# Loads, turns and visits at other places in the order of a linear-attention and feed-forward kernel

## The chip, the cores and the metric

The kernel runs on one core of one Trainium2 chip. The metric is device time in microseconds. A core has TensorE (PE, matmuls), VectorE (DVE), ScalarE (ACT), GpSimd (POOL) and SyncE (SP), each with an instruction stream of its own that it executes in order, and DMA queues that POOL, SP and ACT issue to. Matmuls write to PSUM.

## The reference

Linear attention with decay, in blocks of 64 positions (batch 4, 8 heads, 768 positions, head size 64), and behind it a feed-forward layer on 3072 tokens (512 to 2048 to 512):

```python
intra = np.einsum('bhic,bhjc->bhij', qb, kb) * Dmask[None]
intra = np.einsum('bhij,bhjd->bhid', intra, vb)
inter = np.einsum('bhid,bhde->bhie', qb * lam_pow[None], kv_state)
out[:, :, sl] = intra + inter
kv_state = lam_block[None, :, None, None] * kv_state + np.einsum('bhsd,bhse->bhde', kb_dec, vb)
...
h = x @ w_in
sp = np.where(h > 20.0, h, np.log1p(np.exp(np.minimum(h, 20.0))))
g = h * np.tanh(sp)
return (g @ w_out).astype(np.float32)
```

x is the attention's output, with the heads of a position side by side.

## The kernel before

The kernel cuts the positions into blocks of 128. A chunk is one batch's block with all eight heads; chunk i has block n = i // 4 and batch i % 4, so there are 24 chunks, four to each of six blocks. A block's four chunks together are 512 tokens. For each chunk k, q and v are loaded from DRAM as 16-bit numbers by POOL (`load_k` L70, `load_q` L85, `load_v` L88). The decay is folded into the keys and into the output: `scale_k` (L306) multiplies the keys by a power of the decay, on POOL for chunks 4 to 19, and writes `ktil`.

The chunks are turned (transposed) in two ways. For chunks 0 to 7, `first_t` transposes on TensorE (L228); ScalarE copies the keys out (`pkT`, L237) and VectorE the queries (`pqT`, L246). Then `first_s` computes scores (L262) and masks, and `first_o` the output. From chunk 8 on, `turn` scales on POOL and has SP issue two DMA transposes (L315), which write `qraw` and `kraw`. Such chunks are taken two at a time, as a pair, in a visit: `pair_s` has the scores (L367) and the part of the output that comes from the state (L373); VectorE masks the scores (L382). Some units later `pair_o` has the rest of the output (L394), VectorE empties it (`xtok`, L400), and SP issues transposes of it into `xt` (L404), the input of the feed-forward layer. `pair_a` brings the state up to date: `state_half` for each two chunks (L331), VectorE adds the old state, POOL multiplies by the decay (`wc`, L347).

The feed-forward layer is dense work for TensorE, cut into units of four wide matmuls. For a block, `mm1_unit` (L423) makes one of 16 slices of h in a `ph` buffer of PSUM and ScalarE applies the activation (`hsg`, L430). `mm2_unit` (L455) is a quarter of one batch's output in a `po` buffer; after the fourth, ScalarE copies it to `osb` (L473) and issues the write to DRAM. `ph` and `po` have two buffers each; `pS`, `pk`, `pO`, `pq` one.

The order is written out by hand. First come chunks 0 to 3 and the 16 mm1 units of block 0, with chunks 4 to 7 between them at the units that a table `steps` gives (L556). Then block 1's mm1 work is done in tiles by chunk (L441), with more of chunks 4 to 7 and the turn of chunk 8; then chunks 9 to 11 are turned. The loop of L583 follows. Its first turn, n = 1, is the double period: 32 units, the mm2 units of blocks 0 and 1. Each further turn, n = 2 to 5, has the 16 mm1 units of block n and then its 16 mm2 units. Between the units of a turn stand the two visits of block n + 1 (visit 0 for its chunks 0 and 1, visit 1 for its chunks 2 and 3), and the loads and turns of block n + 2, each put by `at(u, ...)` behind unit u. In the double period the visits are at units 9 and 16, their second steps at 13 and 20.

`behind` is a copy of one element on POOL (`tick`, L411). It reads what a unit has produced, and since POOL executes in order, what follows it on POOL is not issued before that unit has come so far. Semaphores between producers and consumers are put in by the framework.

Of the kernel before, what the change touches and what calls it, by code (L numbers as in the profile page):

```python
# [13 lines left out]
def bc(ap, axis, n):  # L14
    shape = list(ap.shape)
    shape.insert(axis, n)
    return ap.unsqueeze(axis).broadcast_to(shape)
# [3 lines left out]
def kernel(  # L21
# [11 lines left out]
    B, H, S, D = q.shape  # L33
# [6 lines left out]
    NKI = DF // 128  # L40
# [3 lines left out]
    NT = 2  # L44
# [27 lines left out]
    def load_q(i):  # L72
        if i == 0:
            qn[i] = const.tile([128, H, D], F32, name="qn0")
            nc.scalar.dma_start(out=qn[i], in_=chunk_rows(q, i))
            return
        if i < B:
            qn[i] = const.tile([128, RS, D], F16, name=f"qn{i}")
            n, b = divmod(i, B)
            nc.gpsimd.dma_start(  # L80
                out=qn[i].rearrange("p r c -> p (r c)"),
                in_=q[b, :, n * C : (n + 1) * C, :].rearrange("h (s r) c -> h s (r c)", r=RS))
            return
        qn[i] = loads.tile([128, H, D], F16, name="qn", tag="qn")
        nc.gpsimd.dma_start(out=qn[i], in_=chunk_rows(q, i))  # L85
# [23 lines left out]
    def win_t(ni, kc):  # L109
        w = DF // WS // 128  # L110
        t, o = (win0[min(ni, 2)], max(ni - 2, 0)) if ni < w else (win[ni // w], ni % w)
        return t[:, kc, o * 128 : o * 128 + 128]
# [211 lines left out]
    def state_half(n, h, spare, bufs=2):  # L324

        pv = ps.tile([128, 2, JP, D], F32, name="pv", tag=spare, bufs=bufs)
        for x in range(2):
            i = n * B + 2 * h + x
            for j in range(JP):
                for t in range(2):  # L330
                    nc.tensor.matmul(  # L331
                        pv[64 * t : 64 * t + 64, x, j, :], ktil[i][:, 2 * j + t, :],
                        vz[i % NVB][:, 2 * j + t, 0:D], start=True, stop=True)
        rows = [slice(64 * t, 64 * t + 64) for t in range(2)]
        own = [wst[rs, 2 * h : 2 * h + 2, :, rs] for rs in rows]
        if n == 0:
            for rs, o in zip(rows, own):
                nc.vector.tensor_tensor(
                    out=o, in0=pv[rs], in1=bc(bc(lbc[rs, :], 1, 2), 3, D), op=ALU.mult)
            return  # L340
        raw = work.tile([128, 2, JP, D], F32, name="raws", tag="raws", bufs=2)
        if n == 1:
            for rs, o in zip(rows, own):
                nc.vector.tensor_tensor(out=raw[rs], in0=pv[rs], in1=o, op=ALU.add)
        else:
            nc.vector.tensor_tensor(out=raw, in0=pv, in1=wcp[h][n % 2], op=ALU.add)  # L346
        nc.gpsimd.tensor_tensor(  # L347
            out=wcp[h][(n + 1) % 2], in0=raw, in1=bc(bc(lbc, 1, 2), 3, D), op=ALU.mult)
# [61 lines left out]
    def behind(src):  # L410
        nc.gpsimd.tensor_copy(tick, src)  # L411

    hsg = [None] * NG
# [3 lines left out]
    def mm1_part(n, ni, lo, hi):  # L417

        if lo == 0:
            ph_t[ni] = ps.tile([128, GT], F32, name="ph",  # L420
                               tag="ph", bufs=2)
        for kc in range(NKC):
            nc.tensor.matmul(ph_t[ni][:, lo:hi], win_t(ni, kc), xt[n][:, kc, lo:hi],  # L423
                             start=(kc == 0), stop=(kc == NKC - 1))

    def mm1_unit(n, ni):
        if hsg[n] is None:
            hsg[n] = work.tile([128, NKI, GT], F16, name="hsg", tag="hsg", bufs=2)
        mm1_part(n, ni, GT - C if ni in ph_t else 0, GT)
        nc.scalar.activation(hsg[n][:, ni, :], ph_t.pop(ni), AF.Mish)  # L430
# [29 lines left out]
    last_out = [None]  # L460
# [66 lines left out]
    first_s(3)  # L527
    busy(2)
    mm1_part(0, 0, 0, GT - C)
    first_o(3)  # L530
    mm1_part(0, 1, 0, GT - C)
    scale_k(0)
    scale_k(1)
# [19 lines left out]
    load_wout(3)  # L553
    load_k(2 * B)
    load_q(2 * B)
    steps = {11: ((first_t, 4),), 13: ((first_s, 4),), 14: ((first_t, 5), (first_o, 4)), 15: ((first_s, 5),)}  # L556
    for u in range(NKI):
        mm1_unit(0, u)
        if u in (1, 3):
            state_half(0, u // 2, "po")  # L560
        if u == 6:
            nc.vector.tensor_scalar(out=maskT, in0=rel, scalar1=0.0, scalar2=None, op0=ALU.is_ge)
        if u in (6, 7, 8, 10):
            i = {6: 4, 7: 5, 8: 6, 10: 7}[u]
            nc.vector.memset(vz[i][:, :, D : 2 * D], 0.0)
        for f, c in steps.get(u, ()):
            f(c)
    g = 2 * B
    for c in (g + 1, g + 2, g + 3):
        load_k(c)  # L570
        load_q(c)
    steps = {(4, 0): ((first_t, 6),), (4, 1): ((first_o, 5), (first_s, 6)), (4, 2): ((first_t, 7),),
             (4, 3): ((first_o, 6), (first_s, 7)), (5, 1): ((first_o, 7),),
             (6, 1): ((state_half, 0), (turn, g)), (6, 2): ((state_half, 1),)}
    for c in range(B, 2 * B):
        for s in range(WS):
            mm1_tile(c, s)
            for f, i in steps.get((c, s), ()):
                f(*((1, i, "po") if f is state_half else (i,)))
    for f, i in ((turn, 1), (load_v, 0), (turn, 2), (load_v, 1), (turn, 3), (load_v, 2), (load_v, 3)):  # L580
        f(g + i)

    for n in range(NT - 1, NG):  # L583
        dense = [(mm2_unit, m, b, part) for m in ((0, 1) if n < NT else (n,))
                 for b in range(B) for part in range(WS)]
        if n >= NT:
            dense = [(mm1_unit, n, ni) for ni in range(NKI)] + dense
        todo = {}

        def at(u, f, *args):  # L590
            todo.setdefault(u, []).append((f, args))

        if n + 1 < NG:
            pairs = []
            for b in (0, 2):
                s = Pair()
                s.n, s.b = n + 1, b
                pairs.append(s)
            steps = (((9, pair_s, 0), (13, pair_o, 0), (16, pair_s, 1), (20, pair_o, 1),
                      (24, pair_a, 1)) if n < NT else  # L600
                     ((4, pair_s, 0), (8, pair_o, 0), (13, pair_s, 1), (17, pair_o, 1),
                      (20, pair_a, 1)))
            for u, f, b in steps:
                at(u, f, pairs[b])
        if n == NT:
            at(0, lambda: behind(hsg[n][0:1, 0, 0:1]))
            at(0, turn, (n + 1) * B + 2)
            at(0, turn, (n + 1) * B + 3)
        if n + 2 < NG:
            c = (n + 2) * B  # L610
            loads_ = [(f, c + b) for b in range(B) for f in (load_k, load_q)]
            loads_ += [(load_v, c + b) for b in range(B)]
            for x, (f, i) in enumerate(loads_):
                if n >= NT:
                    u = (1, 2, 3, 5, 6, 8, 10, 11, 12, 13, 14, 15)[x]
                    at(u, lambda u=u: behind(hsg[n][0:1, u, 0:1]))
                else:
                    u = 7 + x // 2 * 4
                    if x % 2 == 0:
                        at(u, lambda: behind(last_out[0][0:1, 0:1]))  # L620
                at(u, f, i)
            for b, u in enumerate((21, 23) if n < NT else (18, 19, 21, 23)):
                at(u, turn, c + b)
        for u, (fn, *args) in enumerate(dense):
            fn(*args)
            if u == 0 and late:
                late.pop()()
            for f2, args in todo.get(u, ()):
                if args and isinstance(args[0], Pair):
                    args[0].spare = "po" if u < NKI - 1 and n >= NT else "ph"  # L630
                f2(*args)
# [30 lines left out]
```

## Time and profile before

| | |
|---|---|
| median of three runs | 263.37 us |
| the three runs | 209.98, 263.37, 299.13 us |
| the profiled execution | 210.82 us |
| its span, first to last instruction | 209.0 us |
| TensorE busy | 202.3 us, 97% |
| POOL, ACT, DVE busy | 98.7, 87.2, 67.8 us |
| granted TensorE clock | 1.000 |

The span is shorter than the execution by what lies around it. A row in order of time gives start, length, engine, line, operation, tiles out and in, shapes, and how many were merged; idle time of the engine before it and what ended it stand in brackets. Matmuls overlap, so the time that one costs is read from start to start.

### The profile page before, as it was taken

To read this page: it belongs to the slowest core of one execution; us is meant where nothing else is said; L and a number is where in the kernel's file an instruction comes from. 1 tells how busy PE (TensorE), PEld (TensorE's weight loads), DVE (VectorE), ACT (ScalarE), POOL (GpSimd) and SP (SyncE) were. 2 spreads that over 40 slices of the span, in tenths; PEclk is the share of its full clock that TensorE was granted. 3 is DMA by queue.
4 is the path that set the end of the run, shared out by engine and by line. 5 is a ranking of instruction groups with operands and counts; after the bars stand their busy time and mean duration, and the time that the engine had idled before them with its cause. 6 is when DMAs were issued, how large, how long until landed. Compare 5 with 4: busy or idle time off the path is not lost.

```text
span 209.0 us, 4353 instructions
## 1 busy us (share of the span) xinstructions
PE 202.3 (97%) x1790; PEld 110.1 (53%) x1790; DVE 67.8 (32%) x123; ACT 87.2 (42%) x151; POOL 98.7 (47%) x143
## 2 busy tenths in 40 slices
PE   7999999999999899999999999999999999999993
PEld 4565448999545454445544455544455544444442
DVE  7679516505006522042630042681043600000000
ACT  5865666665311111456312456211556221666120
POOL 7998179944994358796873176840000000000000
PEclk9999999999999999999999999999999999999999
DMA  8999999999999999999996799997702083100112
GB/s 125 141 167 202 185 142 96 157 190 168 145 200 183 193 164 175 217 162 146 136 151 164 186 79 106 133 142 181 171 4 50 2 100 105 50 0 0 53 50 100
DMA packets 107591, 26.78 MB, mean 128 GB/s; under 512 B 99890, under 2 KB 104626, under 8 KB 107570
## 3 DMA queue, kind: packets, MB, share of 16 engines
q0 software_dynamic: 75776, 13.38, 81.8%
q1 hardware_dynamic: 27296, 6.63, 23.2%
q10 hardware_dynamic: 4498, 6.49, 9.5%
q8 instruction: 14, 0.23, 0.5%
q14 instruction: 7, 0.06, 0.1%
HBM read 27.26 MB, written 6.29 MB: 161 GB/s over the span
## 4 chain that ended last, share of the span: by engine, by line
PE 65%; POOL 15%; DMA 15%; issue 2%; SPq 1%; DVE 0%; POOLq 0%
PE po L455 33%; PE ph L423 27%; DMA kn<-in_k_dram 6%; DMA wout<-in_moe_w_out_dram 5%; DMA kraw<-ktil 4%; POOL ktil L306 4%; POOL vz L88 3%; POOL kn L70 2%; PE pS L367 2%; PE pO L394 2%; SPq L315 1%; POOL qn L85 1%; POOL win L101 1%; POOL win L104 1%; POOL wc L347 1%
## 5 line engine op out<-in xcount | busy, mean ns | idle before, releaser
L455 PE MATMUL po<-wout,hsg 128*128 128x512 f16 (+2 forms) x400 | 85.4, 371 | 0.0
L423 PE MATMUL ph<-xt,win 128*128 128x512 f16 (+2 forms) x328 | 72.7, 374 | 0.1
L455 PEld LDWEIGHTS <-hsg 128*128 128x128 f16 x400 | 37.7, 98 | 42.3
L430 ACT ACTIVATE hsg<-ph 128x512 f16<-128x512 f32 x80 | 47.7, 597 | 29.5 <-PE ph L423 29.5
L423 PEld LDWEIGHTS <-win 128*128 128x128 f16 x328 | 30.9, 98 | 35.0 <-issue 0.6
L473 ACT ACTIVATE osb<-po 128x512 f32<-128x512 f32 (+1 forms) x24 | 14.2, 593 | 75.2 <-PE po L455 65.4
L382 DVE TENSOR_TENSOR sb<-pS,maskT 128x512 f16<-128x512 f32 x32 | 20.0, 684 | 57.4 <-PE pS L367 57.4
L70 POOL DMA_DIRECT2D kn<-in_k_dram x23 | 20.9, 907 | 6.9 <-issue 2.3
L88 POOL DMA_DIRECT2D vz<-in_v_dram x24 | 21.7, 905 | 2.0 <-DMA win<-in_moe_w_in_dram 1.0
L85 POOL DMA_DIRECT2D qn<-in_q_dram x20 | 17.9, 896 | 4.9 <-DMA wout<-in_moe_w_out_dram 3.5
L306 POOL TENSOR_TENSOR ktil<-kn,lk 128x512 f16<-128x512 f16 x16 | 16.7, 1050 | 3.8 <-DMA kn<-in_k_dram 3.7
L400 DVE TENSOR_TENSOR xtok<-pO,lqt 128x512 f16<-128x512 f32 x16 | 10.3, 687 | 16.8 <-PE pO L394 16.8
L441 PE MATMUL ph<-xt,win 128*128 128x128 f16 x256 | 15.7, 219 | 0.0
L441 PEld LDWEIGHTS <-win 128*128 128x128 f16 x256 | 14.4, 98 | 0.4
L465 DVE COPY osb<-po 128x128 f32<-128x128 f32 x1 | 0.3, 292 | 38.5 <-PE po L455 38.5
L445 ACT ACTIVATE hsg<-ph 128x512 f16<-128x512 f32 x16 | 9.6, 597 | 6.9 <-PE ph L441 6.9
L347 POOL TENSOR_TENSOR wc<-raws,lbc 128x512 f16<-128x512 f32 x8 | 8.6, 1095 | 5.2 <-DVE raws L346 5.2
L411 POOL COPY tick<-hsg 1x1 f16<-1x1 f16 x25 | 4.4, 177 | 11.7 <-ACT hsg L430 11.6
L268 DVE TENSOR_TENSOR sb<-pS,maskT 128x512 f16<-128x512 f32 x8 | 5.2, 686 | 4.9 <-PE pS L262 4.9
L176 PE MATMUL busy<-kzero 128*128 128x512 f16 x12 | 5.4, 526 | 1.2 <-DVE kzero L158 1.2
L306 DVE TENSOR_TENSOR ktil<-kn,lk 128x512 f16<-128x512 f16 (+1 forms) x8 | 6.4, 840 | 0.0
L288 PE MATMUL pO<-sb,vz 128*128 128x128 f16 x64 | 5.9, 219 | 0.3
(76 smaller groups left out, 118.2 us busy)
## 6 DMA issues: line engine op xcount, KB each, us to landing
out_dram<-osb ACTq DMA_DIRECT2D x23, 256.0 KB, 2.9
vz<-in_v_dram POOLq DMA_DIRECT2D x24, 128.0 KB, 4.7
kn<-in_k_dram POOLq DMA_DIRECT2D x23, 128.0 KB, 5.3
qn<-in_q_dram POOLq DMA_DIRECT2D x23, 128.0 KB, 5.4
wout<-in_moe_w_out_dram POOLq DMA_DIRECT2D x4, 512.0 KB, 10.1
win<-in_moe_w_in_dram POOLq DMA_DIRECT2D x3, 512.0 KB, 9.2
kn<-in_k_dram SPq DMA_DIRECT2D x1, 256.0 KB, 3.2
qn<-in_q_dram ACTq DMA_DIRECT2D x1, 256.0 KB, 3.9
```

Source lines behind the costliest of these rows:

```text
L70: nc.gpsimd.dma_start(out=kn[i], in_=chunk_rows(k, i))
L85: nc.gpsimd.dma_start(out=qn[i], in_=chunk_rows(q, i))
L88: nc.gpsimd.dma_start(out=vz[i % NVB][:, :, 0:D], in_=chunk_rows(v, i))
L306: (nc.vector if i < B or i >= (NG - 1) * B else nc.gpsimd).tensor_tensor(out=t, in0=kn[i], in1=bc(lk, 2, D), op=ALU.mult)
L347: nc.gpsimd.tensor_tensor(out=wcp[h][(n + 1) % 2], in0=raw, in1=bc(bc(lbc, 1, 2), 3, D), op=ALU.mult)
L382: nc.vector.tensor_tensor(out=s.sb[x][t], in0=pS[x][t], in1=bc(maskT, 1, JP), op=ALU.mult)
L400: nc.vector.tensor_tensor(out=xtok[:, :, :, t, :], in0=s.pO[t], in1=bc(bc(lqj[:, :, t], 1, 2), 3, D), op=ALU.mult)
L423: nc.tensor.matmul(ph_t[ni][:, lo:hi], win_t(ni, kc), xt[n][:, kc, lo:hi], start=(kc == 0), stop=(kc == NKC - 1))
L430: nc.scalar.activation(hsg[n][:, ni, :], ph_t.pop(ni), AF.Mish)
L441: nc.tensor.matmul(ph[:, u, :], win_t(w * s + u, kc), xt[n][:, kc, b * C : (b + 1) * C], start=(kc == 0), stop=(kc == NKC - 1),)
L455: nc.tensor.matmul(po[:, lo:hi], hsg[n][:, ki, b * C : (b + 1) * C], wout[part][:, kk, lo:hi], start=(ki == 0), stop=(ki == NKI - 1),)
L473: nc.scalar.activation(o, i, AF.Copy)
```

## The change

Instructions keep their kind; all but a few `tick` copies keep their number. Six things change:

- The turn of chunk 4 on TensorE (`first_t`) stands behind unit 12 of block 0, before behind unit 11.
- Unit 2 of block 0 takes its PSUM tile from the `po` buffers, before from `ph`.
- The second `state_half` of block 0 takes `pS`, before `po`.
- In the double period the loads of v for chunks 10 and 11, before issued with the turns ahead of it, stand behind the output copy of unit 11, ahead of k and q of chunk 12; k and q of chunks 13, 14 and 15 follow behind units 15, 19 and 23, v of chunks 12 and 13 behind unit 27. Before, k and q of chunk 12 stood behind unit 7. Chunk 13 is turned behind unit 24, before 23.
- In turn n = 2, chunks 14 and 15 are turned behind units 0 and 1 (before both behind 0), and their v is loaded behind unit 2 (before in the double period).
- In turns n = 2, 3 and 4, visit 0 is at units 6 and 10, before 4 and 8. In n = 2 and 3 the loads are at units 4 to 23, before 1 to 15, the last three behind output copies; the turns are at 19, 22, 25 and 28, before 18, 19, 21 and 23.

```diff
             ph_t[ni] = ps.tile([128, GT], F32, name="ph",
-                               tag="ph", bufs=2)
+                               tag="po" if n == 0 and ni == 2 else "ph", bufs=2)
...
-    steps = {11: ((first_t, 4),), 13: ((first_s, 4),), 14: ((first_t, 5), (first_o, 4)), 15: ((first_s, 5),)}
+    steps = {12: ((first_t, 4),), 13: ((first_s, 4),), 14: ((first_t, 5), (first_o, 4)), 15: ((first_s, 5),)}
...
-            state_half(0, u // 2, "po")
+            state_half(0, u // 2, *(("po", 2), ("pS", 1))[u // 2])
...
-    for f, i in ((turn, 1), (load_v, 0), (turn, 2), (load_v, 1), (turn, 3), (load_v, 2), (load_v, 3)):
+    for f, i in ((turn, 1), (load_v, 0), (turn, 2), (load_v, 1), (turn, 3)):
...
-                     ((4, pair_s, 0), (8, pair_o, 0), (13, pair_s, 1), (17, pair_o, 1),
+                     ((6, pair_s, 0), (10, pair_o, 0), (13, pair_s, 1), (17, pair_o, 1),
...
+        def after(u, *todo_):
+            if n >= NT and u < NKI:
+                at(u, lambda: behind(hsg[n][0:1, u, 0:1]))
+            else:
+                at(u, lambda: behind(last_out[0][0:1, 0:1]))
+            for f, i in todo_:
+                at(u, f, i)
+
         if n == NT:
-            at(0, lambda: behind(hsg[n][0:1, 0, 0:1]))
-            at(0, turn, (n + 1) * B + 2)
-            at(0, turn, (n + 1) * B + 3)
+            c = (n + 1) * B
+            after(0, (turn, c + 2))
+            after(1, (turn, c + 3))
+            after(2, (load_v, c + 2), (load_v, c + 3))
         if n + 2 < NG:
...
+            if n < NT:
+                after(11, (load_v, c - 2), (load_v, c - 1), (load_k, c), (load_q, c))
...
+            else:
...
+                for u, (f, i) in zip((4, 5, 7, 8, 10, 11, 13, 14, 15, 19, 19, 23), loads_):
+                    after(u, (f, i))
-            for b, u in enumerate((21, 23) if n < NT else (18, 19, 21, 23)):
+            for b, u in enumerate((21, 24) if n < NT else (19, 22, 25, 28)):
                 at(u, turn, c + b)
```

On TensorE, around unit 11 of block 0, the order before is this (`ph_557` is unit 11, `pk_563` and `pq_570` the turn of chunk 4, `ph_577` unit 12, `ph_583` unit 13, `pS_589` the scores of chunk 4; of each step one row is shown):

```order
L423 MATMUL ph_557<-xt_249,win2_81 128x512
...
L228 MATMUL pk_563<-ident_89,ktil_425 128x128
...
L228 MATMUL pq_570<-ident_89,qn_415 128x128
...
L423 MATMUL ph_577<-xt_249,win3_82 128x512
...
L423 MATMUL ph_583<-xt_249,win3_82 128x512
...
L262 MATMUL pS_589<-pqT_575,pkT_568 128x128
```

With the change, at the same place (`ph_563` is unit 12, `pk_569` and `pq_576` the turn, `ph_583` unit 13):

```order
L423 MATMUL ph_557<-xt_249,win2_81 128x512
...
L423 MATMUL ph_563<-xt_249,win3_82 128x512
...
L228 MATMUL pk_569<-ident_89,ktil_425 128x128
...
L228 MATMUL pq_576<-ident_89,qn_415 128x128
...
L423 MATMUL ph_583<-xt_249,win3_82 128x512
...
L262 MATMUL pS_589<-pqT_581,pkT_574 128x128
```

The turn has moved behind unit 12, and one unit is left between it and the scores.

On POOL, at the start of the double period, the order before is this (`ktil_1119` is the scaling of chunk 11, `vz2_71` and `vz3_72` the loads of v for chunks 10 and 11, `osb_1164` the output copy of unit 7, `osb_1235` that of unit 11, `kn_1168` and `qn_1170` are chunk 12, `kn_1239` and `qn_1241` chunk 13):

```order
L306 TENSOR_TENSOR ktil_1119<-kn_666,lk_158 128x512
L88 DMA vz2_71<-in_v_dram 128x8x64
L88 DMA vz3_72<-in_v_dram 128x8x64
L411 CAST tick_167<-osb_1164 1x1
L70 DMA kn_1168<-in_k_dram 128x8x64
L85 DMA qn_1170<-in_q_dram 128x8x64
L411 CAST tick_167<-osb_1235 1x1
L70 DMA kn_1239<-in_k_dram 128x8x64
L85 DMA qn_1241<-in_q_dram 128x8x64
```

With the change (`osb_1228` is the output copy of unit 11, `osb_1277` that of unit 15, `kn_1234` and `qn_1236` are chunk 12, `kn_1281` and `qn_1283` chunk 13):

```order
L306 TENSOR_TENSOR ktil_1119<-kn_666,lk_158 128x512
L411 CAST tick_167<-osb_1228 1x1
L88 DMA vz2_71<-in_v_dram 128x8x64
L88 DMA vz3_72<-in_v_dram 128x8x64
L70 DMA kn_1234<-in_k_dram 128x8x64
L85 DMA qn_1236<-in_q_dram 128x8x64
L411 CAST tick_167<-osb_1277 1x1
L70 DMA kn_1281<-in_k_dram 128x8x64
L85 DMA qn_1283<-in_q_dram 128x8x64
```

Four loads that stood right behind the scaling of chunk 11, two of them behind unit 7, now stand behind unit 11. The order on SP is the same as before.

More of the change, by code (lines that the diff above doesn't have):

```diff
@@ L604 @@
                 at(u, f, pairs[b])
+        def after(u, *todo_):
[5 more added lines that the diff above has]
+                at(u, f, i)
         if n == NT:
-            at(0, lambda: behind(hsg[n][0:1, 0, 0:1]))
-            at(0, turn, (n + 1) * B + 2)
-            at(0, turn, (n + 1) * B + 3)
+            c = (n + 1) * B
+            after(0, (turn, c + 2))
+            after(1, (turn, c + 3))
+            after(2, (load_v, c + 2), (load_v, c + 3))
         if n + 2 < NG:
             c = (n + 2) * B
[L611 to L621, printed above, removed]
-            for b, u in enumerate((21, 23) if n < NT else (18, 19, 21, 23)):
+            if n < NT:
+                after(11, (load_v, c - 2), (load_v, c - 1), (load_k, c), (load_q, c))
+                after(15, (load_k, c + 1), (load_q, c + 1))
+                after(19, (load_k, c + 2), (load_q, c + 2))
+                after(23, (load_k, c + 3), (load_q, c + 3))
+                after(27, (load_v, c), (load_v, c + 1))
+            else:
+                loads_ = [(f, c + b) for b in range(B) for f in (load_k, load_q)]
+                loads_ += [(load_v, c + b) for b in range(B)]
+                for u, (f, i) in zip((4, 5, 7, 8, 10, 11, 13, 14, 15, 19, 19, 23), loads_):
+                    after(u, (f, i))
+            for b, u in enumerate((21, 24) if n < NT else (19, 22, 25, 28)):
                 at(u, turn, c + b)
```

## The prediction

> **What bounds the kernel now.** I read the page first: busy shares, slices and granted clock.
>
> ```profile
> span 209.0 us, 4353 instructions
> PE 202.3 (97%) x1790; PEld 110.1 (53%) x1790; DVE 67.8 (32%) x123; ACT 87.2 (42%) x151; POOL 98.7 (47%) x143
> PE   7999999999999899999999999999999999999993
> PEclk9999999999999999999999999999999999999999
> ```
>
> TensorE is busy nearly everywhere, at the full granted clock in every slice, so a change that takes no work from it can win only its holes. The digits drop in the first slice, around slice 14, and in the last. The busy time by stages says where holes are left (columns after the stretch: length, PE, PEld, DVE, ACT, POOL, clock, DMA share, GB/s):
>
> ```profile
> 21.00:54.00 33.00, 32.51 (x452) 25.06 (x451) 13.22 (x23) 21.19 (x37) 21.93 (x25) 1.00 1.67 156
> 54.00:70.00 16.00, 15.78 (x122) 7.52 (x119) 3.96 (x7) 2.44 (x5) 11.36 (x16) 1.00 1.79 175
> 70.00:85.50 15.50, 14.80 (x133) 7.45 (x134) 4.97 (x8) 1.79 (x3) 10.99 (x15) 1.00 1.59 181
> 85.50:116.00 30.50, 30.50 (x255) 14.95 (x254) 8.83 (x14) 11.94 (x20) 20.89 (x34) 1.00 1.55 165
> 116.00:206.00 90.00, 89.84 (x628) 43.66 (x625) 20.22 (x31) 36.32 (x61) 14.71 (x26) 1.00 0.59 82
> ```
>
> From 21 to 54 us 0.49 us is idle, from 54 to 85.5 us 0.92 us, and from 85.5 to 206 us 0.16 us in 120.5. So after the double period nothing can be won, only lost. TensorE's list in order of time (start, length, then the operation) shows the two holes, and a third that the busy column hides:
>
> ```profile
> 18.02 0.44 PE L331 MATMUL pv<-vz,ktil 128*64 128x64 f16 x16
> 18.55 1.89 PE L423 MATMUL ph<-xt,win 128*128 128x512 f16 x8
> 20.37 0.44 PE L331 MATMUL pv<-vz,ktil 128*64 128x64 f16 x16
> 20.75 7.08 PE L423 MATMUL ph<-xt,win 128*128 128x512 f16 x32
> 28.32 0.40 PE L228 MATMUL pk<-ident,ktil 128*128 128x128 f16 x4 [0.49 <-POOL ktil L306]
> ...
> 28.77 1.89 PE L423 MATMUL ph<-xt,win 128*128 128x512 f16 x8
> ...
> 30.93 1.04 PE L423 MATMUL ph<-xt,win 128*128 128x512 f16 x4
> 31.80 0.39 PE L228 MATMUL pk<-ident,ktil 128*128 128x128 f16 x4
> ...
> 61.98 0.62 PE L367 MATMUL pS<-qraw,kraw 64*128 64x128 f16 x16
> 62.44 0.40 PE L373 MATMUL pO<-wc,qraw 64*128 64x64 f16 x16
> ...
> 69.38 0.40 PE L367 MATMUL pS<-qraw,kraw 64*128 64x128 f16 x8
> 70.70 0.40 PE L367 MATMUL pS<-qraw,kraw 64*128 64x128 f16 x8 [0.92 <-DMA kraw<-ktil]
> 70.94 0.40 PE L373 MATMUL pO<-wc,qraw 64*128 64x64 f16 x16
> 71.27 3.63 PE L455 MATMUL po<-wout,hsg 128*128 128x512 f16 x16
> 74.73 0.63 PE L394 MATMUL pO<-vz,sb 128*128 128x64 f16 x16
> ```
>
> Starts tell more than busy time, since matmuls overlap. Sixteen wide matmuls take from 71.27 to 74.73, 3.46 us or 0.216 us each, and a unit is four of them, 0.865 us. The 32 that start at 20.75 therefore end their issue at 27.67, and the next step starts at 28.32: 0.65 us lost, where 30.93 to 31.80 shows that this change of step alone costs nothing (four times 0.216 is 0.865 of 0.87). At 69.38, sixteen score matmuls should take the 0.46 us of 61.98 to 62.44, but the step behind them starts 1.56 us later: 1.10 us lost. From 18.02 to 18.55 is 0.53 us, where the same sixteen matmuls from 20.37 to 20.75 take 0.38: 0.15 us lost. What lies around the span is 210.82 - 209.0 = 1.82 us, and I leave it.
>
> [...] By the idle column the two marked holes are worth 0.49 + 0.92 = 1.41 us, and less the 0.11 found below the time would be 209.5; by starts they and the third are 1.90 us. [...]
>
> **Chunk 4 turned behind unit 12.** PE waits at 28.32 for POOL's scaled keys of chunk 4. POOL in turn waited for that chunk's load, and the change touches neither:
>
> ```profile
> 27.22 1.04 POOL L306 TENSOR_TENSOR ktil<-kn,lk 128x512 f16<-128x512 f16 x1 [3.72 <-DMA kn<-in_k_dram]
> 30.04 1.06 POOL L306 TENSOR_TENSOR ktil<-kn,lk 128x512 f16<-128x512 f16 x1
> 29.05 0.69 DVE L246 TENSOR_TENSOR pqT<-pq,lq 128x512 f16<-128x512 f16 x1 [5.46 <-PE pq L228]
> ```
>
> They are done at 28.26. With one more unit in front, and 0.15 us won at unit 2, PE arrives at 27.67 - 0.15 + 0.865 = 28.38, when they are ready. The 0.65 us goes. What is late next is the score step of chunk 4, which now has one unit behind the turn instead of two. The turned q is ready 29.74 - 28.32 = 1.42 us after the turn starts. PE comes there after 0.45 (28.32 to 28.77) plus 0.865, 1.31 us, so it waits 1.42 - 1.31 = 0.11 us. The next turn, of chunk 5, would start at 31.80 - 0.65 - 0.15 + 0.11 = 31.11; its keys are ready at 31.10. Term: 0.65 - 0.11 = 0.54 us, with bounds 0.4 (a little lost at chunk 5 too) and 0.65.
>
> **Unit 2 on another bank.** It takes a "po" buffer instead of the third "ph", so it need not wait until ScalarE has read unit 0. The second state half goes to the "pS" bank, which no step uses between the scores of chunk 3 and those of chunk 4. Term: 0.15 us, bounds 0 (something else holds unit 2) and 0.15.
>
> **The double period's loads and turns.** The 1.10 us is a wait for the transposed keys of chunk 11. The chain of waits, then the POOL list, then SyncE's list, then what transposes and loads took from issue to landing (the whole run's kraw; kraw, qraw, vz in their own stretches; kn from 65 to 78 us):
>
> ```profile
> 62.69 7.97 DMA kraw<-ktil
> 59.42 1.81 POOL L88 DMA_DIRECT2D vz<-in_v_dram  x2
> 61.35 0.88 POOL L70 DMA_DIRECT2D kn<-in_k_dram  x1
> 65.43 0.18 POOL L411 CAST tick<-osb 1x1 f16<-1x1 f32 x1 [2.33 <-ACT osb L473]
> 65.89 0.88 POOL L70 DMA_DIRECT2D kn<-in_k_dram  x1 [0.28 <-issue]
> 61.29 1.30 SPq L315 DMA_TRANSPOSE qraw<-qn  x1
> DMA to landing us min/median/max: 2.4/3.2/8.0
> DMA to landing us min/median/max: 4.6/5.5/7.5
> DMA to landing us min/median/max: 3.6/6.0/6.1
> ```
>
> Issued at 62.69, the transpose landed at 70.66, while v of chunks 10 and 11 (two issues from 59.42) and k, q of chunk 12 (from 61.35) were under way. The run's median for such a transpose is 3.2 us. The change puts those four loads behind the output copy of unit 11, so none is issued between the scaling of chunk 11 and about 64.7 us. SyncE's order is the same, and its issue at 62.69 follows from POOL and its own queue. At the median the keys land at 65.9; PE, earlier by 0.54 + 0.15 = 0.69 us, wants them at 69.38 + 0.23 - 0.69 = 68.92, so even 6.2 us is enough. Term: 1.10 us.
>
> What is late next is v of chunk 11, wanted by the output step that stood at 74.73. It now starts at 74.73 - 1.10 - 0.69 = 72.94, and chunk 11 is its second half, 73.17. POOL's tick behind unit 11 moves from 65.43 to 64.74; the first load starts 0.46 us behind it as now (65.43 to 65.89), v of chunk 11 is the second, 0.88 later: 66.08. That leaves 7.1 us. Loads of v from 56 to 62 us took 4.6 to 7.5 us, loads of k from 65 to 78 us 3.6 to 6.1. I take 6.0: nothing added. Behind the waiting tick on POOL stand only the loads and, ten units on, the scaling of chunk 12, so its new wait of some 5 us holds up nobody else.
>
> **Later periods.** Visit 0 two units later, turns spread to units 19 to 28, v loads behind mm2 copies: I cost them at nothing.
>
> ```profile
> 94.08 0.63 PE L394 MATMUL pO<-vz,sb 128*128 128x64 f16 x16
> 98.96 0.62 PE L367 MATMUL pS<-qraw,kraw 64*128 64x128 f16 x16
> 91.03 1.31 SPq L315 DMA_TRANSPOSE kraw<-ktil  x1
> DMA to landing us min/median/max: 5.7/5.7/5.7
> ```
>
> The tightest is chunk 15, turned early in period 2: its keys were issued at 91.03 and landed 5.7 us later, 96.7, and are wanted at 98.96, 2.2 us to spare. Its scaling now follows unit 1 rather than unit 0, but it stood second in POOL's line anyway, so it moves with PE. The last turn, behind unit 28, is wanted behind unit 13 of the next period, 17 units or 14.7 us on; scaling 1.06, two issues of 1.3 and the worst landing of 8.0 make 11.7. The visits now stand three units apart from output step 0 to visit 1, 2.6 us against the 4.9 of 94.08 to 98.96 now; VectorE must have emptied the two accumulators by then, two operations of about the 0.69 us of the pqT row. If such a cover failed it would fail in each of three periods, about 1 us each.
>
> **Sum.** 0.54 + 0.15 + 1.10 = 1.79 us; 210.82 - 1.79 = 209.03, so 209.0. The runs shown have a median of 263.37, from 209.98 to 299.13. The profiled execution stands beside the fastest, 0.4% above it, and 20% below the median; the trace, with the full clock throughout, holds nothing that would make 50 us, so the forecast is for an undisturbed execution.
>
> **Rivals.** *The transpose is late for another reason* (0.12): it is held by its own queue and by output writes, which stay. For it: SyncE issues it right behind the one of 61.29, both on one queue, and an output write leaves at that time too. Against it: the run's median of 3.2, with the same queue and the same writes. Then the keys still land at 70.66, PE resumes at 70.70 as now, and everything won before is swallowed there: 210.8.
>
> *v of chunk 11 is late* (0.08), which ends on the slower side. With a landing time L the loss is L - 7.1: nothing up to 7.1, 0.4 at 7.5, the whole gain at 8.9, and beyond that slower than before. The longest transpose under load took 8.0, giving 209.9; with L = 10 it is 211.9, and 2% slower would need L = 13. For it: four loads are queued in a row, and transposes of x compete. [...]
>
> *A cover fails in every later period* (0.04): 1 us in each of three gives 212.0, 2 us each 215.
>
> *The comparison is off by itself* (0.09), the three runs shown being as far apart as they are: 0.06 to the faster side, as the median lies far above the fastest, 0.03 to the slower.
>
> **Numbers.** The forecast's own case has the remaining 0.67, from 208.2 (the fastest run shown less the sum) to 209.5. The range is 208.0 to 211.4: it takes in the first rival with the 0.6 us or so by which executions differ, and the second up to L = 9.5; 0.67 + 0.12 + 0.05 = 0.84 lie within. A measurement of this kernel can tell about 2%, 4.2 us. Faster by that would be 206.6, which no case of the trace reaches, as all holes together give 1.90: 0.06, from the last rival. Slower, 215.0: 0.03 from it, 0.02 from late v, 0.02 from the periods: 0.07. Within: 0.87.
>
> **What would show it.** Right: no idle before the chunk 4 turn, a score step of chunk 4 that waits 0.1 us, unit 2 starting 0.38 us after the state half, no wait in visit 1 of the double period, the keys of chunk 11 landing within about 4 us, and PE without holes from there. Wrong: an idle PE at the second output step waiting for vz, at visit 1 still waiting for kraw, or small repeated holes in the periods behind.

## The result, and the profile after

| | before | changed |
|---|---|---|
| median of 16 runs | 210.16 us | 209.14 us |
| runs, lowest to highest | 209.34 to 212.01 us | 208.76 to 209.67 us |
| profiled execution | 210.82 us | 209.13 us |
| its span | 209.0 us | 207.3 us |

The ratio is 0.9948, with a 95% interval of 0.9928 to 0.9968: a gain of half a per cent, within the 2% that was called no change. Two of the 16 runs of before, 299.13 us and the 263.37 us that was the first median, are disturbed ones and are left out of the range and of the ratio, as such runs are in the ratios further down; medians are of all runs. The profiled executions lie 1.69 us apart, the medians 1.02 us. The experiments below are mostly about that difference.

On the page of the changed kernel, the summary by engine of the chain that ended last:

```profile
PE 91%; DVE 0%; issue 0%
```

The same line of the kernel before, and some of the pieces of its chain in order of time:

```profile
PE 65%; POOL 15%; DMA 15%; issue 2%; SPq 1%; DVE 0%; POOLq 0%
14.62 12.46 DMA kn<-in_k_dram
...
27.22 1.04 POOL ktil L306
28.26 0.89 POOL qn L85
...
61.29 1.30 SPq L315
...
62.69 7.97 DMA kraw<-ktil
...
70.70 0.40 PE pS L367 x8
```

From the load of chunk 4's keys to visit 1 the chain of before went over DMA, POOL and SyncE, and not over TensorE's first hole.

The changed kernel's busy time by stages (length, PE, PEld, DVE, ACT, POOL, clock, DMA share, GB/s):

```profile
21.00:54.00 33.00, 33.00 (x454) 25.32 (x453) 13.31 (x23) 21.22 (x37) 21.96 (x26) 1.00 1.66 157
54.00:70.00 16.00, 16.00 (x145) 8.04 (x144) 4.47 (x8) 2.39 (x4) 10.49 (x13) 1.00 1.61 169
70.00:85.50 15.50, 15.50 (x116) 7.43 (x114) 4.36 (x7) 2.98 (x5) 10.97 (x15) 1.00 1.90 196
85.50:116.00 30.50, 30.50 (x255) 15.01 (x254) 8.84 (x14) 11.39 (x20) 22.53 (x37) 1.00 1.91 162
```

The idle 0.49 and 0.92 us are gone: TensorE is busy without a break from 21 to 116 us, and the chain runs over TensorE alone from early on. TensorE's list in order of time, at the places of the three holes:

```profile
18.25 0.44 PE L331 MATMUL pv<-vz,ktil 128*64 128x64 f16 x16
18.62 1.90 PE L423 MATMUL ph<-xt,win 128*128 128x512 f16 x8
...
20.83 7.94 PE L423 MATMUL ph<-xt,win 128*128 128x512 f16 x36
28.61 0.39 PE L228 MATMUL pk<-ident,ktil 128*128 128x128 f16 x4
...
29.06 1.03 PE L423 MATMUL ph<-xt,win 128*128 128x512 f16 x4
30.07 0.40 PE L262 MATMUL pS<-pqT,pkT 64*128 64x128 f16 x8
...
68.87 0.62 PE L367 MATMUL pS<-qraw,kraw 64*128 64x128 f16 x16
69.33 0.40 PE L373 MATMUL pO<-wc,qraw 64*128 64x64 f16 x16
...
73.12 0.63 PE L394 MATMUL pO<-vz,sb 128*128 128x64 f16 x16
```

Unit 2 starts 0.37 us after the state half (before 0.53). The 36 matmuls from 20.83 and the turn of chunk 4 follow each other without a gap. The sixteen score matmuls of visit 1 stand in one row, 0.46 us from the step behind them (before 1.56). All of it starts 0.23 us later than before (18.25 against 18.02): the start of the kernel, which the change does not touch, took that much longer in this execution.

POOL's list and SyncE's list in the double period, then the time from issue to landing of the transposed keys of chunk 11 (issued at 63.11) and of v of chunk 11 (the second of the two issues from 65.26):

```profile
64.85 0.18 POOL L411 CAST tick<-osb 1x1 f16<-1x1 f32 x1 [4.96 <-ACT osb L473]
65.26 1.82 POOL L88 DMA_DIRECT2D vz<-in_v_dram  x2 [0.24 <-issue]
63.11 2.15 SPq L315 DMA_TRANSPOSE kraw<-ktil  x1
DMA to landing us min/median/max: 4.4/4.4/4.4
DMA to landing us min/median/max: 4.1/4.1/4.1
```

POOL now idles 4.96 us before the tick. The keys land 4.4 us after their issue in place of 8.0, at 67.5, and are wanted at 69.1 (their scores are the second half of the row at 68.87, 0.23 later). v of chunk 11 is issued at 66.2, lands at 70.3 and is wanted at 73.12 + 0.23 = 73.35: 3 us to spare.

### The profile page after: what moved, and what is told of

The parts are those of the page before. It is cut to its first block, busy times and chain, and to the rows that moved or that the text cites. A ratio compares the mean times of both kernels' runs of the same rounds, so it can differ in the third digit from the quotient of the medians.

```text
span 207.3 us, 4355 instructions
## 1 busy us (share of the span) xinstructions
PE 202.1 (97%) x1790; PEld 110.5 (53%) x1790; DVE 68.8 (33%) x123; ACT 87.0 (42%) x151; POOL 100.1 (48%) x144
## 4 chain that ended last, share of the span: by engine, by line
PE 91%; DVE 0%; issue 0%
PE po L455 40%; PE ph L423 34%; PE ph L441 7%; PE pS L367 2%; PE pO L394 2%; PE pv L331 2%; PE pO L288 1%; PE pO L373 1%; PE pS L262 1%; PE pk L228 0%; PE pO L284 0%; PE pq L228 0%; DVE osb L465 0%; DVE ktil L306 0%
## 5 line engine op out<-in xcount | busy, mean ns | idle before, releaser
L411 POOL COPY tick<-hsg 1x1 f16<-1x1 f16 x21 | 3.7, 176 | 10.2 <-ACT hsg L430 10.0
L411 POOL CAST tick<-osb 1x1 f16<-1x1 f32 x11 | 2.4, 219 | 12.7 <-ACT osb L473 12.7
L306 DVE TENSOR_TENSOR ktil<-kn,lk 128x512 f16<-128x512 f16 (+1 forms) x8 | 7.2, 944 | 0.0
```

Source lines behind the costliest of these rows:

```text
L306: (nc.vector if i < B or i >= (NG - 1) * B else nc.gpsimd).tensor_tensor(out=t, in0=kn[i], in1=bc(lk, 2, D), op=ALU.mult)
```

## The experiments

The theory: the transposed keys of chunk 11 are late because four loads are under way beside them, and while they are late, whatever TensorE wins before visit 1 is lost again there. The rivals: the keys are late for their own queue and the output writes; or each hole counts for itself and the three terms simply add. Ratios are to the kernel before, run beside each.

| kernel | median, us | ratio | 95% interval |
|---|---|---|---|
| changed, second time | 209.15 | 0.9954 | 0.9923 to 0.9984 |
| early edits alone | 211.02 | 1.0032 | 1.0000 to 1.0064 |
| the same, second time | 210.22 | 0.9989 | 0.9950 to 1.0028 |
| the same, third time | 210.54 | 0.9999 | 0.9951 to 1.0047 |
| double period's loads alone | 209.37 | 0.9955 | 0.9927 to 0.9982 |
| only k, q of chunk 12 later | 209.40 | 0.9968 | 0.9941 to 0.9995 |
| only v of 10 and 11 later | 209.36 | 0.9952 | 0.9922 to 0.9982 |
| early edits, k, q of 12 later | 209.33 | 0.9957 | 0.9932 to 0.9983 |
| changed, later periods as before | 209.24 | 0.9954 | 0.9930 to 0.9978 |
| changed, v behind unit 15 | 211.80 | 1.0078 | 1.0043 to 1.0113 |
| before, once more | 211.13 | 1.0023 | 0.9983 to 1.0064 |
| before, two output writes left out | 209.59 (one run) | | |

The kernel before against itself, 1.0023, shows what such a ratio can be without any edit.

**The early edits alone.** The kernel before with these lines:

```diff
-                               tag="ph", bufs=2)
+                               tag="po" if n == 0 and ni == 2 else "ph", bufs=2)
...
-    steps = {11: ((first_t, 4),), 13: ((first_s, 4),),
+    steps = {12: ((first_t, 4),), 13: ((first_s, 4),),
...
-            state_half(0, u // 2, "po")
+            state_half(0, u // 2, *(("po", 2), ("pS", 1))[u // 2])
```

> The kernel before with the two early edits alone: chunk 4 turned behind unit 12, unit 2 on the po buffers and the second state half on pS. Theory: holes one and three go (no idle before the turn of chunk 4, 0.37 us from state half to unit 2), TensorE reaches visit 1 of the double period 0.7 to 0.8 us earlier, but the keys of chunk 11 land when they did, so the wait there grows by what was won: its idle time 0.9 plus 0.7, and the time moves by no more than 0.3 us (209.8 to 210.2 where before has 210.16). Rival, each hole counts for itself: 0.7 us faster, 209.4, with a wait at visit 1 as before.

> The two early edits alone once more, since the first profile of them is of its slowest kind (span 211.9) and 12 runs went from 209.91 to 214.45. Theory: what TensorE wins before visit 1 is swallowed there, and more than that: loads that are tied to TensorE's units (k and q of chunk 13 behind unit 11) start earlier while the transposes of chunk 11 don't, so the keys land later. Expected: a wait of 1 to 3 us at visit 1 again, k of chunk 13 issued near 65.1 (65.89 in the kernel before), median 0 to 1 us above before. Rival, chance of that run: the wait is 0.5 to 1 us and the median is at or below before.

> The two early edits alone, for a profile like the others (the first had the longest wait of its kind, the second was disturbed as a whole). Theory: no hole at chunk 4 and none at unit 2, and a wait at visit 1 of 1 to 2 us, longer than the 0.8 and 1.1 us in the two profiles of the kernel before by about what was won ahead of it; span 208.3 to 209.3. Rival, each hole counts for itself: the wait is 1 us or less and the span at or below 208.0.

Three ratios, 1.0032, 0.9989 and 0.9999: no gain, and not the loss of up to 1 us that I expected of the second either. The second's profiled execution took 728.48 us and isn't read. In the third profile, TensorE at visit 1, and the landing of the keys issued at 62.33:

```profile
68.88 0.40 PE L367 MATMUL pS<-qraw,kraw 64*128 64x128 f16 x8
70.72 0.40 PE L367 MATMUL pS<-qraw,kraw 64*128 64x128 f16 x8 [1.45 <-DMA kraw<-ktil]
62.33 8.35 DMA kraw<-ktil
```

TensorE comes there 0.50 us earlier than before (68.88 against 69.38; 0.7 to 0.8 was expected) and goes on at 70.72, where before had 70.70: the wait grew from 0.92 to 1.45 us, just by what was won. Both holes ahead were gone, and the span is 209.0 us like before's. So the holes don't count for themselves, as the chain of before already said: it reaches visit 1 past the first of them. That the keys landed within 0.02 us of before's is luck, since they were issued 0.36 us earlier and took 0.38 us longer. The other half of my expectation stays open: in the third run k of chunk 13 was issued at 65.4, half a microsecond earlier than before, and the keys took 8.4 us in place of 8.0 but landed at 70.68, no later. In the first profile they did land later, at 72.01, after 8.6 us, but there SyncE had issued them later too, at 63.44.

**The double period's loads alone.** The changed kernel without the early edits, and with the tables of the later periods as before:

```diff
-                     ((6, pair_s, 0), (10, pair_o, 0), (13, pair_s, 1), (17, pair_o, 1),
+                     ((4, pair_s, 0), (8, pair_o, 0), (13, pair_s, 1), (17, pair_o, 1),
...
-                for u, (f, i) in zip((4, 5, 7, 8, 10, 11, 13, 14, 15, 19, 19, 23), loads_):
+                for u, (f, i) in zip((1, 2, 3, 5, 6, 8, 10, 11, 12, 13, 14, 15), loads_):
...
-            for b, u in enumerate((21, 24) if n < NT else (19, 22, 25, 28)):
+            for b, u in enumerate((21, 24) if n < NT else (18, 19, 21, 23)):
```

> The kernel before with the loads and turns of the double period as changed (v of chunks 10 and 11 and k, q of chunk 12 behind unit 11, the rest as it follows, v of 14 and 15 in period 2), but without the two early edits and with the loads, turns and visits of the later periods as before. Theory: no wait at visit 1, the transposed keys of chunk 11 land within 5 us of their issue, holes one and three stay (0.65 and 0.15 us). The gain is the wait that before has there: 1.1 us in the profiled execution; the runs of before and after lie only 1.02 us apart, which less the 0.8 of the early edits leaves 0.2 to 0.4 us at the median, and the runs lie closer together than those of before (2.7 us from the lowest to the highest undisturbed one). Rival, the transpose is late for its own queue and the output writes: the wait stays, no gain.

The gain is 0.94 us at the median (210.31 to 209.37), nearly that of the whole change, and the runs lie between 209.08 and 210.22. That is more than the 0.2 to 0.4 expected, since I had taken the early edits to bring their full 0.8. TensorE's list shows why they don't, with the landing of the keys of chunk 11, issued at 61.61, below it:

```profile
18.33 0.44 PE L331 MATMUL pv<-vz,ktil 128*64 128x64 f16 x16
18.86 1.89 PE L423 MATMUL ph<-xt,win 128*128 128x512 f16 x8
...
21.06 7.08 PE L423 MATMUL ph<-xt,win 128*128 128x512 f16 x32
27.97 0.39 PE L228 MATMUL pk<-ident,ktil 128*128 128x128 f16 x4
...
69.03 0.62 PE L367 MATMUL pS<-qraw,kraw 64*128 64x128 f16 x16
69.48 0.40 PE L373 MATMUL pO<-wc,qraw 64*128 64x64 f16 x16
DMA to landing us min/median/max: 4.5/4.5/4.5
```

The third hole is there (0.53 us from 18.33 to 18.86), visit 1 has no wait, but the hole at chunk 4 isn't there either, although the turn still stands behind unit 11. POOL's list has the reason:

```profile
25.91 1.04 POOL L306 TENSOR_TENSOR ktil<-kn,lk 128x512 f16<-128x512 f16 x1 [2.45 <-DMA kn<-in_k_dram]
```

The keys of chunk 4 had landed before 25.91, 1.3 us earlier than in the profile of before (27.22), with the same instructions ahead of them.

**The kernel before, profiled again**, without an edit.

> The kernel before itself, a second profile. Theory: two of the three holes change from one execution to the next, since what they wait for lands at other times (the keys of chunk 4 landed between 25.8 and 27.2 us in six profiles, and the hole stands only where they come after about 26.5). Expected: hole one 0 to 0.3 us with chunk 4 landing before 26.5, or again some 0.6 if it lands at 27; hole three 0.15 as before; the wait at visit 1 between 0.3 and 3 us. Rival: the holes are those of the first profile to 0.1 us.

```profile
20.76 7.08 PE L423 MATMUL ph<-xt,win 128*128 128x512 f16 x32
28.30 0.40 PE L228 MATMUL pk<-ident,ktil 128*128 128x128 f16 x4 [0.46 <-POOL ktil L306]
...
69.36 0.40 PE L367 MATMUL pS<-qraw,kraw 64*128 64x128 f16 x8
70.34 0.40 PE L367 MATMUL pS<-qraw,kraw 64*128 64x128 f16 x8 [0.59 <-DMA kraw<-ktil]
```

The hole at chunk 4 is back, almost as in the first profile (0.62 us by starts), and the wait at visit 1 is a third shorter. Over 13 profiles (all but the second of the early edits), with the same loads ahead of them, the keys of chunk 4 landed between 25.8 and 27.5 us, eight times before 26.5. Without the edit TensorE gets there between 27.7 and 28.2 us, and POOL needs 1.2 us after the landing (27.08 to 28.32 in the first profile of before), so a hole needs a landing after 26.5 to 27.0: of the six profiles without the edit, the two of before have it.

The two waits hang together. In the five profiles with late keys of chunk 4, POOL scaled chunk 11 at 58.0 to 58.8 us, in seven of the other eight at 57.1 to 57.9 (once at 58.6), and SyncE issued the transposed keys of chunk 11 3.8 to 4.8 us behind that. In the chain of before shown above, POOL hands the lateness of the first load on to visit 1; that it does so in each of the others isn't shown.

**Which loads.** The kernel before with only k and q of chunk 12 behind unit 11, and with only v of chunks 10 and 11 behind it:

```diff
-                    u = 7 + x // 2 * 4
+                    u = 11 if x < 2 else 7 + x // 2 * 4
```

```diff
-    for f, i in (..., (turn, 3), (load_v, 2), (load_v, 3)):
+    for f, i in (..., (turn, 3)):
...
+                if n < NT and x == 2:
+                    at(u, load_v, c - 2)
+                    at(u, load_v, c - 1)
```

> The kernel before with only k and q of chunk 12 moved from unit 7 to unit 11 of the double period; v of chunks 10 and 11 stay at the turns. Theory, all four loads share the 16 DMA engines with the transpose: half of the load is gone, the keys of chunk 11 land some 1.5 to 2.5 us earlier (68 to 69 us in place of 70.7), and the wait at visit 1 is below 0.3 us; time as that of the double period's loads alone. Rival, the two v loads are what holds it: the wait stays near 1 us. Rival, loads do not matter: the same.

> The kernel before with only v of chunks 10 and 11 moved behind unit 11, ahead of k and q of chunk 13; k and q of chunk 12 stay behind unit 7, where POOL now waits for the unit's output copy. Theory, what is under way beside the transposes counts, whichever load it is: k and q of chunk 12 are issued some 1 us earlier than before (near 60.5) and are half the load, so the keys of chunk 11 land within 5 to 6.5 us of their issue and the wait is below 0.3 us, as with k and q alone moved; ratio 0.995 to 0.998. Rival, k and q of chunk 12 are what holds them: the wait stays near 1 us, ratio 0.999 to 1.002.

Either pair alone is enough: 0.9968 and 0.9952, and no wait at visit 1. The landing of the keys of chunk 11, in the first (issued at 61.39) and then in the second kernel (at 61.97):

```profile
DMA to landing us min/median/max: 6.0/6.0/6.0
DMA to landing us min/median/max: 6.3/6.3/6.3
```

With all four loads it is 8.0 (before, twice) to 8.6 (the early edits), with none 4.5 (the loads alone), 4.4 and 3.7 (the changed kernel, twice), 4.2 (later periods as before) and 3.6 (v behind unit 15), with two in between. It falls with the number of loads under way, whichever they are, while queue and order on SyncE are the same in all of them, so the keys' own queue alone doesn't hold them. The earlier issue helped as well (the first kernel's keys came at 67.4, where I had expected 68 at the earliest): at 8.0 us from it the keys would have come 0.4 and 0.7 us late here, not 1.1. That k and q were issued 1 us earlier, as I had expected of the second kernel, was not so: 61.21 against 61.35.

**Early edits and k, q of chunk 12 later.** The first edit above on top of the early edits.

> The two early edits with only k and q of chunk 12 moved behind unit 11; v of chunks 10 and 11, and all that follows, as before. Theory: that is enough to clear visit 1 (with k and q alone moved, the keys landed 6.0 us after their issue, in time), but TensorE comes 0.2 to 0.8 us earlier, so a wait of up to 0.5 us comes back in some executions: 209.1 to 209.5, ratio 0.995 to 0.998. Rival, v must move too once TensorE is early: a wait near 1 us, ratio near 1.

0.9957, without a wait at visit 1 in its profile. The keys landed 7.3 us after their issue there, more than in the two kernels above with as many loads, but they were issued early, at 61.47. Nothing is left for the rest of the change to bring that these runs could tell.

**Output writes left out**, with the loads as before (the first two writes of block 0, so that part of the output is not written; one run):

```diff
+        if n == 0 and b < 2:
+            return
         late.append(lambda: queue.dma_start(out=out[r0 : r0 + C, lo:hi], in_=osb))
```

> The kernel before without the writes of the output of block 0's batches 0 and 1 (so a part of the output is left unwritten); the loads stay. It tells whether the output writes hold the transposes of chunk 11. Theory, the loads do: the keys still land 6 us or more after their issue and visit 1 waits as before. Rival, the writes do: they land within 5 us and there is no wait.

```profile
DMA to landing us min/median/max: 7.5/7.5/7.5
```

The keys still take 7.5 us, so it isn't these two writes that hold them. A third write, issued at 65.2 while the keys are under way, stays here; the changed kernel has it too, at 64.8, and its keys took 4.4 us. Visit 1 had no wait all the same, since SyncE issued the keys at 61.64, a microsecond earlier than in the first profile; the point of issue moves from one execution to the next (61.3 to 63.4 us in the 13 profiles), and the wait with it. In those profiles the chain that ended last passes through the transposed keys in four, the two of before and the two of the early edits, and in none of the rest.

**The new deadline from its other side.** The changed kernel with v of chunks 10 and 11 behind unit 15:

```diff
-                after(11, (load_v, c - 2), (load_v, c - 1), (load_k, c), (load_q, c))
-                after(15, (load_k, c + 1), (load_q, c + 1))
+                after(11, (load_k, c), (load_q, c))
+                after(15, (load_v, c - 2), (load_v, c - 1), (load_k, c + 1), (load_q, c + 1))
```

> The changed kernel with v of chunks 10 and 11 behind unit 15 of the double period in place of unit 11, ahead of k and q of chunk 13. It measures the other side of the new deadline. In the changed kernel v of chunk 11 was issued at 66.2, landed at 70.3 and was wanted at 73.35. Four units later it is issued near 70.2; with a landing of 4 to 7 us it lands at 74.3 to 77.3, and TensorE waits 0.9 to 3.9 us at the second output step for it: 210 to 213 us. Rival, the landing is fast enough or the masks are later still: no wait, 209.1.

```profile
69.50 3.63 PE L455 MATMUL po<-wout,hsg 128*128 128x512 f16 x16
74.31 0.39 PE L394 MATMUL pO<-vz,sb 128*128 128x64 f16 x8 [1.18 <-DMA vz<-in_v_dram]
75.19 0.39 PE L394 MATMUL pO<-vz,sb 128*128 128x64 f16 x8 [0.48 <-DMA vz<-in_v_dram]
```

The output step should start 3.46 us after 69.50, at 72.96, and its second half 0.23 later; the second half starts at 75.19, 2.0 us late, for v of chunk 11. The kernel is slower than before, 1.0078. So the place behind unit 11 is right, and one output copy later is too late.

**The later periods as before.** The tables of the edit shown at the loads alone, in the changed kernel with its early edits. The first three units of period 2 stay as changed.

> The changed kernel with the loads, turns and visits of the later periods (n = 2, 3, 4) put back to the units of before. Theory: they cost nothing and bring nothing: time within 0.2 us of the changed kernel (209.14), no hole behind 70 us. Rival, the spread of the later loads and the later first visit matter: more than 0.4 us slower, with holes at the visits of periods 2 to 4.

0.9954 against 0.9948 and 0.9954: the same. What these tables change in periods 2 to 4 is worth nothing that can be measured.

**The changed kernel again.**

> The changed kernel again beside its parts, on the same chip. Theory: ratio 0.994 to 0.996, as before; against the double period's loads alone (0.9955) it is 0 to 0.3 us faster, since chunk 4 and unit 2 add only what their holes cost in an average execution. Rival, the parts add up: 0.8 us faster than the loads alone, ratio below 0.993.

0.9954, and 0.22 us below the median of the loads alone (of another set of runs), inside both intervals. The parts do not add up.

## Why the prediction was right, and where a term was mis-sized

The forecast was 209.0 us within 208.0 to 211.4, most likely no change to within 2%; measured were 209.14 us and a ratio of 0.9948.

*Chunk 4 turned behind unit 12* (0.54 us). The mechanism is as told. The score step behind it waits 0.05 us (29.06 to 30.07 is 1.01, less 0.865 and the 0.10 that the same change of step took from 28.77 to 30.60 before), not 0.11. But the hole that it closes is one of some executions only: four of the six profiles with the turn where it was ran without it.

*Unit 2* (0.15 us): 0.53 became 0.37, as told.

*The double period* (1.10 us): the wait is gone in every profile with those loads moved. The transposes took 4.4 us and not the run's median of 3.2, which did not matter. The size depends on the execution: 1.10 and 0.76 us by starts in two profiles of the same kernel. The loads alone gained 0.94 us at the median.

*The wait for v of chunk 11*: issued at 66.2 where 66.08 was forecast, landed after 4.1 us where I took 6.0. The limit of 7.1 us held on its other side: issued at 70.01 and landing after 5.1 us (75.15), the formula gives 70.01 - 66.08 + 5.1 - 7.1 = 1.9 us of loss, and 2.0 was measured. An early issue did not pay for these loads: issued earlier, they delayed a transfer that was wanted sooner (8.0 us against 4.4), and only the run behind unit 15 shows a loss by a late issue.

*Later periods at nothing*: so it was.

*The sum* (1.79 us) is the step that was mis-sized as a gain. Between the two profiled executions it is 1.69, and 1.92 when the 0.23 us later start is set aside. Between the medians it is 1.02. I made the sum against one execution of before that had the hole at chunk 4 and a wait of 1.1 us at visit 1, and that stood 0.66 us above its kernel's median of 210.16. A gain read off as 1.79 us would have been too large by three quarters at the median. The time came out right because the changed kernel shows almost none of these holes in either of its profiles: what is left is TensorE's own work, which the trace gave correctly. The spread tells the same: 2.7 us from the lowest to the highest run of before in the first table, 0.9 with the change (in its second set eleven of twelve runs lay within 0.6 us, and one at 211.13).

*The first rival*, a transpose that is late for another reason, with all gains swallowed at visit 1, was wrong in its cause and right in its mechanism: with the loads left in place, that is just what the early edits did. The prediction kept this swallowing for the rival alone, though it holds whenever the keys are late.

That the late keys are late because of the loads under way beside them is shown by the counts of loads; whether it is DMA engines, queues or memory that they share, no run here tells. Why the keys of chunk 4 land up to 1.7 us apart in executions that are alike up to there stays open as well.

## What to carry to other kernels

A hole on the bounding engine is worth something only if no later wait ends at a time that this engine doesn't set (the early edits alone closed two holes, and came to 1.0032, 0.9989 and 0.9999); look for the last wait that hangs on a transfer, and clear that one first. When loads delay a transfer that is wanted soon (here 8.0 us against 4.4), move those that have time to spare behind it, but work out the new deadline of each: four units of slack made the difference between half a per cent gained and most of one lost. And when a gain is read from the waits of one profiled execution, profile the kernel a second time, or compare that execution with the median: a wait on a transfer may not be there in the next one (the hole at chunk 4 stood in two of the six profiles without the edit). The chain that ended last tells beforehand which holes count: closing one that it passes by wins nothing while the chain stands.

## What was not expected of the hardware

In the first profile of the early edits alone the wait at visit 1 was 3.09 us by the idle column. TensorE's list, and the busy time by stages (with the granted clock behind POOL's column):

```profile
68.56 0.40 PE L367 MATMUL pS<-qraw,kraw 64*128 64x128 f16 x8
72.05 0.61 PE L367 MATMUL pS<-qraw,kraw 64*128 64x128 f16 x8 [3.09 <-DMA kraw<-ktil]
```

```profile
68.00:71.90 3.90, 0.96 (x11) 0.32 (x9) 1.29 (x2) 0.40 (x1) 1.93 (x3) 1.00 1.87 190
71.90:75.40 3.50, 3.35 (x30) 1.76 (x31) 1.29 (x2) 0.00 (x0) 0.00 (x0) 0.52 1.60 197
75.40:80.00 4.60, 4.60 (x36) 2.33 (x35) 1.29 (x2) 0.60 (x1) 1.67 (x3) 1.00 0.99 115
```

Behind it the granted clock was 0.52 for 3.5 us, and then 1.00 again. The waits of 1.45 us in the third profile and of 1.18 and 0.48 with v behind unit 15 had no such sequel: the mean granted clock of their executions was 0.997 and 0.999, and 0.992 in this one. Whether the wait is what lowered the clock, and from what length on it does, this one profile doesn't show. If it is, the wait cost more than its length: 3.5 us at a clock of 0.52 are 3.5 x 0.48, an estimate of some 1.7 us, which the prediction's straight line for a late load left out. With v behind unit 15, four of the ten runs have a mean clock of 0.992 too and took 212.38 to 213.26 us, where the other six took 210.96 to 211.83; of the 86 runs of the changed kernel and of those with some of the four loads moved and v in time, none has it. No trace of those four was kept, so a wait near 3 us behind them would fit, and is not shown.
